# Two small reorderings in a TensorE-bound attention kernel: a piece of the last tile moved ahead, and keys computed by weight chunk in both branches

## Chip, cores, metric

One core of one Trainium2 chip. The metric is the device time of one execution in microseconds (us); lower is better. "PE" is the tensor engine, "ACT" ScalarE, "DVE" VectorE, "SyncE" the engine that issues most of the DMAs.

## The reference

Two linear-attention blocks A and B read the same x (2048 x 640, bf16), each with its own weights, and are mixed by a gate.

```python
g = sigmoid((x * gate_w).sum(-1, keepdims=True))
# for X in (A, B); H = 32 heads of 20:
q, k, v = split_heads(x @ wqkv)
phi = lambda t: where(t > 0, t + 1, exp(t)) + 1e-6
kv  = einsum("bhsd,bhse->bhde", phi(k), v);  z = phi(k).sum(over s)
o   = (phi(q) @ kv) / (phi(q) @ z + 1e-6)
out_X = o @ wo
out = g * out_A + (1 - g) * out_B
```

The kernel folds kv and wo into one 640 x 640 matrix per branch (WPA, WPB; "the projection"), so that the output of a tile of 128 rows is two products, one per branch, and the scaling by 1/den and by the gate goes onto phi(q). The folded matrix is written out to HBM and read back to get another layout.

## The kernel before

The program lists operations; a small list scheduler inside it picks the order on each engine other than PE from estimated times. PE keeps the program's order. Cuts are marked.

The loads at the start, all on the SyncE queue except x's tile 1 and small ones. `xt_dma` is a transposing load of x^T; x^T of tiles 0 and 1 is made by PE itself.

```python
ld_x("ACT", 1)
...
for c in range(NC):                 # NC = 5 chunks of 128 rows of the key weights
    if c == 0:
        ld_x("SP", c)
    ld_wk("SP", "A", c)             # 160 KB each
xt_dma(2, 3)
for c in range(NC):
    ld_wk("SP", "B", c)
for t0, t1 in ((3, 4), (4, 5), (5, 6), (6, 8), (8, 12), (12, 16)):
    xt_dma(t0, t1)
```

The keys. One `k_step` is one weight chunk for one tile: a matmul of 512 and one of 128 or 129 columns. `k_unit` is five steps and the evaluation of phi.

```python
warm(4); warm(1, 2)                 # matmuls on ones, to have PE busy
pss = [Buf("k", "ps", 2) for _ in range(2)]
x_tp(0); warm(1, 1); x_tp(1)        # x^T of tiles 0, 1 on PE
for c in range(2):
    for t in range(2):
        k_step("A", t, c, pss[t])
gate_col()
for c in range(2, NC):
    for t in range(2):
        k_step("A", t, c, pss[t])
...                                 # k_post of both
k_unit("A", 2)
for t in range(3):
    k_unit("B", t)
for t in range(3, NT):
    for X in XS:
        k_unit(X, t)
```

The end. A's part of tiles 0 to 14 is computed while B's projection is on its way, copied to SBUF, and later added to B's part. Tile 15 has both parts at the very end.

```python
for t in range(8, NOA): o_part(t)   # NOA = 15: A's parts; B's projection is being stored and loaded
...
for t in range(NOA): o_rest(t)      # B's parts, added to A's by DVE, stored
...
def out_last(t):                    # t = 15
    for lo, hi, eng in ((0, 512, "ACT"), (512, D, "DVE")):
        ps = Buf("o", "ps")
        for X in XS:
            o_mm(X, t, ps, lo, hi)
        o_post(t, ps, lo, hi, eng, ...)
```

## Time and profile before

| | before |
|---|---|
| time, median (range) of the first 3 runs | 188.17 us (188.03 to 188.83) |
| span of the profiled run | 186.8 us |
| PE busy | 184.0 us (98%) |
| DVE, ACT busy | 74%, 51% |
| PE's waits once the keys have begun | 0.35 us before B's weight chunks, 0.45 us before B's projection |

PE is nearly always busy, so only its short waits can be had. The prediction shows the lines and how the two numbers in the last row come out of the start times of matmuls. A busy share alone would have said that nothing is left.

### The profile page before, as it was taken

The page shows a single profiled execution, that of the slowest core. Times are in us where ns is not written, and L with a number is a line of the kernel's source. Part 1 is how long each engine was busy: PE and PEld are TensorE (multiplying, and loading weights), DVE is VectorE, ACT ScalarE, POOL GpSimd, SP SyncE. Part 2 cuts the span into 40 slices and gives each one's busy share as a digit, 9 for nine tenths or more (in the row PEclk, how much of TensorE's full clock was granted, in tenths as well). Part 3 has the DMA queues.
Part 4 walks back from the last instruction along what each step waited for, and adds up shares of the span by engine and source line. Part 5 has one row for each costly group of instructions (what it writes and reads, how often), then busy time and mean ns, then how long its engine had stood idle before and what let it go on. Part 6 is the DMA issues. An engine that isn't in the chain of part 4 may idle for free.

```text
span 186.8 us, 3273 instructions
## 1 busy us (share of the span) xinstructions
PE 184.0 (98%) x1297; PEld 106.6 (57%) x1297; DVE 137.4 (74%) x264; ACT 95.2 (51%) x167; POOL 0.8 (0%) x10
## 2 busy tenths in 40 slices
PE   9999999999999999999999999999999999999995
PEld 4555555555555556555557555555566555555552
DVE  2388888888833555487799999998899996368652
ACT  5455655556554546544675666887633775300001
POOL 1000000000000000000000000000000000000000
DMA  6999999994001011010701412025426256523433
GB/s 190 291 163 163 266 394 362 338 200 114 4 0 35 0 39 35 0 35 20 100 2 35 84 33 50 14 62 154 175 41 115 58 131 164 143 105 107 142 107 105
DMA packets 36501, 21.38 MB, mean 114 GB/s; under 512 B 25694, under 2 KB 36230, under 8 KB 36486
## 3 DMA queue, kind: packets, MB, share of 16 engines
q1 hardware_dynamic: 36044, 20.96, 44.4%
q8 instruction: 10, 0.16, 0.4%
q10 hardware_dynamic: 442, 0.21, 0.4%
q14 instruction: 5, 0.04, 0.1%
HBM read 10.87 MB, written 4.26 MB: 81 GB/s over the span
## 4 chain that ended last, share of the span: by engine, by line
PE 92%; DMA 4%; ACT 2%; issue 0%; DVE 0%; SPq 0%; DVEq 0%
PE ps L795 23%; PE ps L536 19%; PE ps L641 18%; PE ps L955 18%; PE ps L642 5%; PE ps L537 5%; DMA WPB<-wpsB 3%; DMA wpsB<-WKW 2%; PE ps L703 2%; PE ps L467 1%; ACT WKW L753 1%; PE ps L738 1%; ACT PKB L979 1%; PE ps L480 1%; DVE TSB L999 0%
## 5 line engine op out<-in xcount | busy, mean ns | idle before, releaser
L536 PE MATMUL ps<-WKW,XT 128*128 128x512 bf16 x160 | 44.6, 382 | 0.0
L812 ACT ACTIVATE EK<-ps 128x512 bf16<-128x512 f32 x40 | 23.9, 598 | 30.1 <-PE ps L795 29.9
L537 PE MATMUL ps<-WKW,XT 128*128 128x128 bf16 (+1 forms) x160 | 35.3, 220 | 0.0
L569 ACT ACTIVATE EK<-ps 128x640 bf16<-128x640 f32 x32 | 22.4, 704 | 10.3 <-DVE EK L572 5.4
L536 PEld LDWEIGHTS ps<-WKW,XT 128*128 128x128 bf16 x160 | 15.7, 98 | 19.6 <-DMA WKW<-in_B_wqkv_dram 0.7
L795 PE MATMUL ps<-XT,WQA 128*128 128x512 bf16 x100 | 24.5, 379 | 0.0
L795 PE MATMUL ps<-XT,WQB 128*128 128x512 bf16 x100 | 23.8, 380 | 0.0
L641 PE MATMUL ps<-XN,PKA 128*128 128x512 bf16 x80 | 23.5, 379 | 0.0
L641 PE MATMUL ps<-XN,PKB 128*128 128x512 bf16 x80 | 23.5, 379 | 0.0
L822 DVE TENSOR_SCALAR EK<-EK 128x512 bf16<-128x512 bf16 x40 | 11.6, 289 | 13.5 <-ACT EK L812 13.3
L642 PE MATMUL ps<-XN,PKA 128*128 128x129 bf16 x80 | 17.6, 220 | 0.0
L642 PE MATMUL ps<-XN,PKB 128*128 128x129 bf16 x80 | 17.6, 220 | 0.0
L955 PE MATMUL ps<-WPA,EX 128*128 128x512 bf16 x120 | 17.0, 299 | 0.0
L955 PE MATMUL ps<-WPB,PKA 128*128 128x512 bf16 x120 | 16.5, 299 | 0.3 <-DMA WPB<-wpsB 0.3
L795 PEld LDWEIGHTS ps<-XT,WQB 128*128 128x128 bf16 x100 | 10.9, 118 | 8.6 <-issue 0.4
L537 PEld LDWEIGHTS ps<-WKW,XT 128*128 128x128 bf16 x160 | 15.8, 98 | 0.0
L572 DVE TENSOR_SCALAR EK<-EK 128x640 bf16<-128x640 bf16 x32 | 10.4, 326 | 7.2 <-ACT EK L569 7.1
L795 PEld LDWEIGHTS ps<-XT,WQA 128*128 128x128 bf16 x100 | 10.6, 117 | 8.1
L641 PEld LDWEIGHTS ps<-XN,PKA 128*128 128x128 bf16 x80 | 9.4, 117 | 7.9
L641 PEld LDWEIGHTS ps<-XN,PKB 128*128 128x128 bf16 x80 | 9.4, 117 | 7.9
L580 DVE SCALAR_TENSOR_TENSOR PKA<-ps,EK 128x640 bf16<-128x640 f32 x16 | 13.2, 825 | 0.5
L580 DVE SCALAR_TENSOR_TENSOR PKB<-ps,EK 128x640 bf16<-128x640 f32 x16 | 13.2, 825 | 0.6
(77 smaller groups left out, 222.8 us busy)
## 6 DMA issues: line engine op xcount, KB each, us to landing
out_dram<-TSB SPq DMA_DIRECT2D x15, 160.0 KB, 1.8
XN<-in_A_x_dram SPq DMA_DIRECT2D x1, 2240.0 KB, 8.9
WKW<-in_A_wqkv_dram SPq DMA_DIRECT2D x5, 160.0 KB, 3.9
WKW<-in_B_wqkv_dram SPq DMA_DIRECT2D x5, 160.0 KB, 3.6
WQA<-in_A_wqkv_dram SPq DMA_DIRECT2D x1, 800.0 KB, 10.6
WQB<-in_B_wqkv_dram SPq DMA_DIRECT2D x1, 800.0 KB, 11.7
WVA<-in_A_wqkv_dram SPq DMA_DIRECT2D x1, 800.0 KB, 12.7
WVB<-in_B_wqkv_dram SPq DMA_DIRECT2D x1, 800.0 KB, 14.5
```

The costliest lines, as they stand in the source:

```text
L536: e.matmul(a[:, 0:512], l, WK[X][:, c, 0:512], start=(c == 0), stop=(c == NC - 1))
L537: return e.matmul(a[:, 512:w], l, WK[X][:, c, 512:w], start=(c == 0), stop=(c == NC - 1))
L569: op("ACT", lambda e: e.activation(EK[:, ek.slot, :], psw(ps, D), ACT.Exp), act_cost(D), ins=[ps] + first, outs=[ek], name="ke")
L572: lambda e: e.tensor_scalar(EK[:, ek.slot, :], EK[:, ek.slot, :], 1.0, EPS, op0=ALU.min, op1=ALU.add),
L580: lambda e: e.scalar_tensor_tensor(PKt[X][:, t, :], psw(ps, D), 0.0, EK[:, ek.slot, :], op0=ALU.max, op1=ALU.add),
L641: e.matmul(a[:, 0:512], l, XN[:, t, 0:512], start=(t == 0), stop=(t == NT - 1))
L642: return e.matmul(a[:, 512 : D + 1], l, XN[:, t, 512 : D + 1], start=(t == 0), stop=(t == NT - 1))
L703: r = e.matmul(PS[0:n, ps.slot, GR * i : GR * i + NC * w], WV[X][:, c, lo : lo + n], gv[:, c, :, 24 * u : 24 * u + w], start=(c == 0), sto ...
L795: r = e.matmul(PS[:, ps.slot, :], WQ[X][:, c, g::5], XT[:, c, 512 * b : 512 * b + 512], start=(c == 0), stop=(c == NC - 1),)
L812: lambda e: e.activation(EQ[:, eq.slot, :], PS[:, ps.slot, :], ACT.Exp),
L822: lambda e: e.tensor_scalar(EQ[:, eq.slot, :], EQ[:, eq.slot, :], 1.0, EPS, op0=ALU.min, op1=ALU.add),
L955: r = e.matmul(a[:, l0 - lo : h0 - lo], PQ[X, b][:, g, 128 * (t % 4) : 128 * (t % 4) + 128], WP[X][:, g, l0:h0], start=(X == first and g = ...
```

## The change

The intent: take both waits out without adding or removing a matmul. A's 512 columns of tile 15 (1.08 us of PE) fill the wait before B's projection. At the start, B's weights go ahead of x^T of tile 2, and B's tiles 0 and 1 share each chunk as it arrives, as A's did already.

```diff
         ld_wk("SP", "A", c)
-    xt_dma(2, 3)
     for c in range(NC):
         ld_wk("SP", "B", c)
-    for t0, t1 in ((3, 4), (4, 5), (5, 6), (6, 8), (8, 12), (12, 16)):
+    for t0, t1 in ((2, 3), (3, 4), (4, 5), (5, 6), (6, 8), (8, 12), (12, 16)):
         xt_dma(t0, t1)
@@ keys
-    k_unit("A", 2)
-    for t in range(3):
-        k_unit("B", t)
-    for t in range(3, NT):
+    pss = [Buf("k", "ps", 2) for _ in range(2)]
+    for c in range(NC):
+        for t in range(2):
+            k_step("B", t, c, pss[t])
+    for t in range(2):
+        k_post("B", t, pss[t])
+    for t in range(2, NT):
         for X in XS:
             k_unit(X, t)
@@ end
-    def out_last(t):
-        for lo, hi, eng in ((0, 512, "ACT"), (512, D, "DVE")):
-            ps = Buf("o", "ps")
-            for X in XS:
-                o_mm(X, t, ps, lo, hi)
+    LAST = ((0, 512, "ACT"), (512, D, "DVE"))
+    blast = [Buf("o", "ps") for _ in LAST]
+
+    def last_a(t):
+        o_mm("A", t, blast[0], 0, 512)
+
+    def last_b(t):
+        for (lo, hi, eng), ps in zip(LAST, blast):
+            if hi == D:
+                o_mm("A", t, ps, lo, hi)
+            o_mm("B", t, ps, lo, hi)
             o_post(t, ps, lo, hi, eng, "ACT" if hi == D else "SP")
@@ order
     for t in range(8, NOA):
         o_part(t)
+    last_a(NT - 1)
@@
-    out_last(NT - 1)
+    last_b(NT - 1)
```

## The prediction

> **What bounds the kernel now.** I read the page first, then the waits of the tensor engine (PE), then PE alone in order of time wherever a wait was named, then the SyncE queue and the landings beside those places.
>
> The page's first part, and from its groups the only PE group with an idle time in front of it:
>
> ```profile
> PE 184.0 (98%) x1297; PEld 106.6 (57%) x1297; DVE 137.4 (74%) x264; ACT 95.2 (51%) x167; POOL 0.8 (0%) x10
> L955 PE MATMUL ps<-WPB,PKA 128*128 128x512 bf16 x120 | 16.5, 299 | 0.3 <-DMA WPB<-wpsB 0.3
> ```
>
> PE is busy for 184.0 of 186.8 us; VectorE (DVE) has 74%, ScalarE (ACT) 51%. The rest of the span is the start (0.39 us) and what follows the last matmul (about 2.1 us, read off the order of time: last matmul done at 184.74, end at 186.8). So only two things can shorten this kernel: less PE work, or the short stretches in which PE waits. The change leaves the number and shapes of the matmuls as they are, so all of it must come from stretches. The list of waits names these for PE and its weight loads:
>
> ```profile
> PEld ps L536 <- DMA WKW<-in_B_wqkv_dram: 0.7, 2, 0.4
> PEld ps L536 <- DMA WKW<-in_A_wqkv_dram: 0.4, 1, 0.4
> PE ps L955 <- DMA WPB<-wpsB: 0.3, 1, 0.3
> ```
>
> Weight loads run beside matmuls, so their 0.7 us isn't 0.7 us of lost time. What was lost shows in the start times of the matmuls (first column; PE in order of time, second unit of keys of branch B):
>
> ```profile
> 8.97 0.38 PE L536 MATMUL ps<-WKW,XT 128*128 128x512 bf16 x1
> 9.19 0.22 PE L537 MATMUL ps<-WKW,XT 128*128 128x129 bf16 x1
> 9.43 0.39 PE L536 MATMUL ps<-WKW,XT 128*128 128x512 bf16 x1
> 9.66 0.22 PE L537 MATMUL ps<-WKW,XT 128*128 128x129 bf16 x1
> 9.86 0.39 PE L536 MATMUL ps<-WKW,XT 128*128 128x512 bf16 x1
> 10.09 0.22 PE L537 MATMUL ps<-WKW,XT 128*128 128x129 bf16 x1
> 10.14 0.38 PE L536 MATMUL ps<-WKW,XT 128*128 128x512 bf16 x1
> ```
>
> These are chunks 2, 3, 4 of B's tile 0 and chunk 0 of tile 1. An undisturbed chunk (512 and 129 columns) takes 0.27 us from start to start, as the steps before 8.97 do. Here the steps are 0.46, 0.43, 0.28: lost are 0.19 and 0.16, together **0.35 us**. The arrivals that the trace records agree: B's five weight chunks are complete at 7.73, 8.19, 8.62, 9.39 and 9.81, and the two late matmuls start at 9.43 and 9.86.
>
> The second place, PE where A's parts of the output end and B's begin:
>
> ```profile
> 156.97 4.24 PE L955 MATMUL ps<-WPA,PKA 128*128 128x512 bf16 x30
> 161.46 3.60 PEld L955 LDWEIGHTS ps<-WPB,PKA 128*128 128x128 bf16 x27 [0.58 <-issue]
> 161.49 3.69 PE L955 MATMUL ps<-WPB,PKA 128*128 128x512 bf16 x26 [0.28 <-DMA WPB<-wpsB]
> ```
>
> The 30 matmuls that start at 156.97 are A's parts of tiles 12 to 14. In the B stage one tile follows another every 1.36 us (the DVE adds start at 164.40, 165.76, 167.12), so the next matmul was due at 156.97 + 3 x 1.357 = 161.04. It starts at 161.49: **0.45 us** lost. The page says 0.28 because it counts a matmul as busy until it has drained, not until the next may start. The chain of waits shows what this matmul is held by:
>
> ```profile
> 152.88 3.61 DMA wpsB<-WKW
> ...
> 156.62 4.73 DMA WPB<-wpsB
> 161.35 0.14 issue
> 161.49 23.27 PE ps L955 x170
> ```
>
> Two transfers, out to HBM and back, hold B's folded projection until 161.35. After it PE has 23.27 us without a wait.
>
> **What the Trainium skill says.** "TensorE: Matmul & The Clock Gate", section "Wait — 56ns, not 53.3ns?": a warm matmul of N columns follows the one before after N / 2.4 GHz + 2.5 ns. That makes 215.8 ns for 512 and 55.8 ns for 128 columns, and 5 x (215.8 + 55.8) = 1.358 us a tile; the trace has 1.36. The same page's "Back-to-back issue gap" calls 131 ns the sustained spacing for N = 512, which this trace doesn't show; I go with the measured spacing. "DMA: Bandwidth & Descriptors", section "Issuing engines are not separate DMA queues": all issuing queues share the same 16 DMA engines. So moving one load behind others on SyncE doesn't create bandwidth, it only changes who is first. The trace agrees: the mean busy share over the first 10 us is 0.91, and A's last three chunks land 0.35 to 0.6 us apart. "PSUM — Partial Sum Buffer", section "Specifications (TRN2)": 8 banks. A tile of 640 columns takes a pair here, and four pairs is all there is.
>
> **The change part by part.**
>
> *1. x^T of tile 2 behind B's weights.* On SyncE the transposing load is issued from 2.81 to 4.13 us, B's five weight loads from 4.18 to 6.64. Taking it out of the way moves all five up by 4.18 - 2.81 = 1.37 us at the issue. Issue to landing was 3.4 to 3.7 us for them. In bytes only one load of 160 KB is passed, which took 0.67 us of landing time (A's last chunk complete at 6.33, x^T at 7.00), so I expect the chunks 0.7 to 1.4 us earlier: chunk 4 at 8.4 to 9.1 instead of 9.81, chunk 0 at 6.4 to 7.0 instead of 7.73.
>
> *2. Keys by weight chunk for tiles 0, 1 in B too.* Today PE does A0 and A1 by chunk (until 7.07), A2 (7.07 to 8.43), then B0. After the change B0 and B1 follow A1 at once, chunk by chunk. So B's chunk 0 is wanted 1.36 us earlier, at 7.07. But a chunk is then used by two tiles, 0.54 us per chunk instead of 0.27: chunks 0 to 4 are wanted at 7.07, 7.61, 8.16, 8.70, 9.25. Against estimated landings of at most 7.0, 7.5, 7.9, 8.7 and 9.1 (each 0.7 earlier than before) all five are in time, if barely at the late end. Both gaps go: -0.35 us. x^T of tile 2 is wanted after those ten steps, at 7.07 + 10 x 0.272 = 9.79. It is issued at about 5.3; before, issue to landing was 4.2 us for it, which makes 9.5; the bound by bytes is 9.81, when everything up to B's chunk 4 had landed in the old order. So it's in time or late by little: I set down +0.05 us. The key units' PSUM pairs: A0's is wanted again at 9.79 and was free once DVE had read it, at 8.93 (8.10 + 0.83). By the same rates (ACT 0.17 + 0.70, DVE 0.33 + 0.82 a unit) B0's is free near 11.7 and wanted at 12.5. No wait from there.
>
> *3. A's 512 columns of tile 15 ahead of B's first tile.* Five matmuls of 512 columns, 5 x 0.216 = 1.08 us, move from the tail (181.86 to 182.94 in the trace) into the wait for B's projection. PE then reaches B's first tile at 161.04 + 1.08 = 162.12 and finds the projection there (161.35 + 0.14). The tail loses 1.08 us, the stretch before gains 1.08 and loses its gap: net -0.45 us. I don't count 1.08. With part 2 the PE work and the projection's whole chain move earlier together by 0.3, since the chain starts from PE's own last small burst at 146.35; the slack of 162.12 - 161.49 = 0.63 us stays. The price is one bank held from there to the end, so B's 15 tiles have three pairs in place of four. An add takes 0.82 us and begins 0.1 us after its tile is done, and the pair is wanted again two tiles (2.7 us) later: even with a 0.81 us scaling ahead of it there's no wait.
>
> *The end.* The last three pieces keep their order: B's 512 columns, both branches' 128 columns, eviction, two stores. All of it moves forward unchanged.
>
> Sum: -0.35 + 0.05 - 0.45 = **-0.75 us** of 188.17, so **187.4 us**, 0.4% faster.
>
> **The rivals.**
>
> *A. The new load order only trades one wait for another.* B's first chunk is wanted at 7.07 now, and x^T of tile 2 comes 2.5 us later at the issue. For it: DMA is full in those microseconds, and margins are tenths. Against: the bytes ahead of B's chunks fall, and each chunk now feeds twice as much PE time. If chunks come only 0.4 earlier and x^T at 10.2, 0.3 to 0.5 us returns: 187.8.
>
> *B. The wait for B's projection is shorter or longer in other executions than in the profiled one.* The gain of part 3 is the gap, up to 1.08 us. If the gap is usually 0.1, gain 0.4 in all (187.75); if usually above 1.0, gain up to 1.4 (186.8). The three times lie 0.8 us apart, so such a variation can't be excluded.
>
> *C. Something is reshuffled.* The kernel's own list scheduler fixes the order on DVE, ACT and SyncE from simulated times; a small shift early, or a bank held late, can put a transposing load ahead of the stores of B's projection (such a load took 1.2 to 1.6 us of SyncE). Of that, 0.63 us is covered; the rest would show. Against: the order of the last transposes is pinned in the code. This would make 188.2 to 189.
>
> *D. The full 1.08 us comes off the tail.* It would if PE were idle for as long before B's first tile; the trace has 0.45. 186.8.
>
> **Range and chances.** The centre is 187.4. A with 15 to 20%, B either way with some 25%, C with 10% widen it to 186.9 to 188.1 for 8 in 10. A change of 2% is 3.8 us; no wait of PE in this trace adds up to that, and no rival costs it. Faster 0.01, same 0.98, slower 0.01.
>
> **What would show it.** Right: no step above 0.3 us between the key matmuls' starts from 7.07 to 12.5; five matmuls of A's projection on their own directly before the first with B's; no idle time before these; the B stage still at 1.36 us a tile; the last matmul done near 184.0. Wrong, and in what way: a weight load waiting for x^T near 9.8 (A), a first B tile that still waits for its projection (B or C), an add that PE waits for in the last 25 us (the held bank).

## The result, and the profile after

| | before | after |
|---|---|---|
| median (range) of 6 runs each | 188.20 us (188.03 to 188.83) | 188.01 us (187.62 to 188.41) |
| ratio, 95% interval | | 0.9987 (0.9966 to 1.0008) |
| span of the profiled run | 186.8 us | 186.7 us |

A ratio is the mean time of one kernel's runs over that of the other's of the same rounds, so not quite the ratio of the medians quoted. The time is inside the predicted range, but the difference is 0.25 us (means 188.30 and 188.05) where 0.75 was forecast, and the interval allows at most 0.64.

Yet the trace shows what was forecast. First PE's waits of the kernel after, the whole list; the one at the top is before the keys begin, the other is for x's tile 0. (ps is the accumulator in PSUM that is written, WKW the key weights, XT x^T; L466 is line 466 of that run's kernel, so the same statement is L535 in one kernel and L536 in another.)

```profile
PE ps L466 <- DVE ONE L383: 0.4, 1, 0.4
PE ps L479 <- DMA XN<-in_A_x_dram: 0.2, 1, 0.2
```

No weight chunk of B and no projection is waited for. PE in order of time where A's parts end and B's begin (start, duration, instruction, count):

```profile
157.23 5.32 PE L957 MATMUL ps<-WPA,PKA 128*128 128x512 bf16 x34
162.17 3.85 PEld L957 LDWEIGHTS ps<-WPB,PKA 128*128 128x128 bf16 x28
162.39 3.91 PE L957 MATMUL ps<-WPB,PKA 128*128 128x512 bf16 x27
```

A's tiles 12 to 14 are followed by the five extra matmuls (34 in the list: 35 less one record that is missing), and B's first matmul follows without an idle mark, 162.39 - 157.23 = 5.16 us later, which is 3 x 1.357 + 1.08 = 5.15. From A's tile 12 to the end of the last matmul it is 27.33 us, and 27.77 before: -0.44 us, as forecast (-0.45).

So the loss must be at the start. The first 512-column key matmuls of the kernel after:

```profile
3.84 0.63 PE L535 MATMUL ps<-WKW,XT 128*128 128x512 bf16 x1
4.38 0.63 PE L535 MATMUL ps<-WKW,XT 128*128 128x512 bf16 x1
4.91 0.63 PE L535 MATMUL ps<-WKW,XT 128*128 128x512 bf16 x1
5.44 0.63 PE L535 MATMUL ps<-WKW,XT 128*128 128x512 bf16 x1
6.05 0.39 PE L535 MATMUL ps<-WKW,XT 128*128 128x512 bf16 x1
```

A matmul that takes 0.63 us rather than 0.38 is read here as one at half clock: its step takes 0.53 us rather than 0.27. (The granted clock reads 1.00 all the same, so the durations are the only sign.) Here four are slow; in the trace before two were, at 3.65 and 4.18. That costs 2 x 0.26 = 0.52 us, and the keys began 0.19 us later (3.84 instead of 3.65), as x's first tile came later (2.58 instead of 2.39). In all, A's tiles 0 and 1 are done 0.59 us later than in the trace before (the weight load of the eleventh step, the first after them, starts at 7.63 instead of 7.04); it isn't the full 0.71 because PE had lost about 0.1 us there to A's own chunks. From there to the end the trace after is 0.76 us shorter, as forecast. The Trainium skill, "TensorE: Matmul & The Clock Gate", section "What's actually happening", says that PE's clock is released after a window of sustained work, that this window runs free of the kernel's start, and that the point of release varies by half a microsecond from run to run. The traces agree that it varies, but more widely (below).

Three theories of the front part followed. **Chance**: the clock's release is luck, equal for both kernels, and both gains are real in every run. **Absorbed**: weights arrive at fixed times, so a late clock lets them arrive unnoticed; the 0.35 us wait exists only in early-clock runs of the kernel before, and the front part of the change gains less on average. **Caused**: the change itself makes the start later.

### The profile page after: what moved, and what is told of

Same layout as the page of the kernel before. It is cut to its first block, busy times and chain, and to the rows that moved or that the text cites. A ratio compares the mean times of both kernels' runs of the same rounds, so it can differ in the third digit from the quotient of the medians.

```text
span 186.7 us, 3247 instructions
## 1 busy us (share of the span) xinstructions
PE 182.6 (98%) x1272; PEld 107.1 (57%) x1297; DVE 137.2 (73%) x264; ACT 95.0 (51%) x167; POOL 0.8 (0%) x10
## 4 chain that ended last, share of the span: by engine, by line
PE 97%; DMA 1%; issue 1%; DVE 0%; DVEq 0%
PE ps L957 23%; PE ps L797 23%; PE ps L535 18%; PE ps L643 18%; PE ps L536 5%; PE ps L644 5%; PE ps L705 2%; DMA XN<-in_A_x_dram 1%; PE ps L740 1%; PE ps L479 1%; DVE TSB L1001 0%; PE ps L466 0%; DVEq L237 0%; PE ps L516 0%
## 5 line engine op out<-in xcount | busy, mean ns | idle before, releaser
L535 PE MATMUL ps<-WKW,XT 128*128 128x512 bf16 x154 | 43.8, 386 | 0.0
L536 PE MATMUL ps<-WKW,XT 128*128 128x128 bf16 (+1 forms) x160 | 35.5, 222 | 0.3
L535 PEld LDWEIGHTS ps<-WKW,XT 128*128 128x128 bf16 x160 | 15.9, 99 | 19.1 <-issue 0.6
L797 PE MATMUL ps<-XT,WQA 128*128 128x512 bf16 x96 | 24.0, 379 | 0.1
L957 PE MATMUL ps<-WPA,EX 128*128 128x512 bf16 (+1 forms) x117 | 16.6, 297 | 0.2
L957 PE MATMUL ps<-WPB,PKA 128*128 128x512 bf16 (+1 forms) x118 | 16.4, 298 | 0.1
L536 PEld LDWEIGHTS ps<-WKW,XT 128*128 128x128 bf16 x160 | 15.9, 99 | 0.0
L579 DVE SCALAR_TENSOR_TENSOR PKA<-ps,EK 128x640 bf16<-128x640 f32 x16 | 13.2, 825 | 0.5
L579 DVE SCALAR_TENSOR_TENSOR PKB<-ps,EK 128x640 bf16<-128x640 f32 x16 | 13.2, 825 | 0.6
```

Source lines behind the costliest of these rows:

```text
L535: e.matmul(a[:, 0:512], l, WK[X][:, c, 0:512], start=(c == 0), stop=(c == NC - 1))
L536: return e.matmul(a[:, 512:w], l, WK[X][:, c, 512:w], start=(c == 0), stop=(c == NC - 1))
L579: lambda e: e.scalar_tensor_tensor(PKt[X][:, t, :], psw(ps, D), 0.0, EK[:, ek.slot, :], op0=ALU.max, op1=ALU.add),
L797: r = e.matmul(PS[:, ps.slot, :], WQ[X][:, c, g::5], XT[:, c, 512 * b : 512 * b + 512], start=(c == 0), stop=(c == NC - 1),)
L957: r = e.matmul(a[:, l0 - lo : h0 - lo], PQ[X, b][:, g, 128 * (t % 4) : 128 * (t % 4) + 128], WP[X][:, g, l0:h0], start=(X == first and g = ...
```

## The experiments

Sixteen runs, each with five timing rounds against the kernel before on the same chip. All results were correct.

### 1. Both kernels again, and each half of the change alone

No edit for `base_again` (the kernel before) and `chg_again` (the kernel after). `tail_only` has only the last two hunks of the diff (end, order), `front_only` only the first two (loads, keys).

> The kernel before, unchanged, to see how its start varies from one execution to the next. In the first trace two 512-column key matmuls ran at half speed (0.63 us each) and PE waited 0.35 us for B's weight chunks; in the trace after the change four ran at half speed (0.53 us more lost) and nothing waited. Theory 'chance' (the clock's release moves from run to run whatever the kernel; both gains are real): ratio 1.000, and among profiles of this kernel some show four half-speed matmuls. Theory 'absorbed' (the arrivals of the weights are fixed in time, so a late clock eats the 0.35 us gap of the kernel before): ratio 1.000, and where four matmuls are slow the gap before B's chunks is gone. Theory 'caused' (the change itself makes the start later): two slow matmuls here again.

Measured: 188.62 us, ratio 1.0007 (0.9982 to 1.0031). Its profile is a late-clock one: matmuls are slow until 6.36. And there is no wait for B's chunks. PE's only waits, complete:

```profile
PE ps L467 <- DVE ONE L383: 0.4, 1, 0.4
PE ps L955 <- DMA WPB<-wpsB: 0.3, 1, 0.3
```

The matmuls around its last slow one, and where B's chunks come in:

```profile
5.27 0.63 PE L536 MATMUL ps<-WKW,XT 128*128 128x512 bf16 x1
5.87 0.59 PE L536 MATMUL ps<-WKW,XT 128*128 128x512 bf16 x1
6.36 0.45 PE L536 MATMUL ps<-WKW,XT 128*128 128x512 bf16 x1
6.71 0.38 PE L536 MATMUL ps<-WKW,XT 128*128 128x512 bf16 x1
...
9.70 0.38 PE L536 MATMUL ps<-WKW,XT 128*128 128x512 bf16 x1
9.97 0.38 PE L536 MATMUL ps<-WKW,XT 128*128 128x512 bf16 x1
10.24 0.38 PE L536 MATMUL ps<-WKW,XT 128*128 128x512 bf16 x1
```

The steps at 9.70, 9.97, 10.24 have the undisturbed 0.27 us. B's chunks 3 and 4 landed at 9.51 and 9.91, as late as in the first trace (9.39, 9.81), but PE reached them later. This is the picture of "absorbed", and it takes "caused" away as the only reason: the kernel before has late starts too.

> The changed kernel, unchanged, in more rounds. 'chance': 0.75 us below the kernel before (ratio 0.996), and a profile with two slow matmuls may show up. 'absorbed': about 0.45 us below (ratio 0.9976), plus 0.35 us only in runs with an early clock. 'caused': about 0.2 us below (0.9987 as measured first), four slow matmuls again and the first key matmul at 3.84 rather than 3.65 us.

Measured: 187.89 us, ratio 0.9986 (0.9949 to 1.0023), no PE wait but for the first two. One of the six runs took 190.14 us; the other five average 187.86. The profiled run wasn't that one, so its reason stays unknown.

> Only A's 512 columns of the last tile ahead of B's first tile; the start is that of the kernel before. By the prediction -0.45 us (the gap before B's projection) in the profile, ratio 0.9976. In the trace after the change the projection came 0.20 us earlier in relation to PE's work, so the gap may vary: -0.25 to -0.45. 'chance' and 'absorbed' say the same here; 'caused' too, since the start isn't touched.

Measured: 188.02 us, 0.9979 (0.9961 to 0.9996). No wait for the projection, and 27.33 us from A's tile 12 to the last matmul again. At the start, B's chunks came late in this trace (the first at 8.53, the last at 10.26), and the steps of B's tile 0 lost 0.68 us to them.

> Only the new load order and the keys of tiles 0 and 1 by chunk in both branches; the old tail. 'chance': -0.35 us less 0.05 (ratio 0.9984). 'absorbed': 0 to -0.35 us by the clock of each run, -0.1 on average (0.9995). 'caused': +0.2 us or more (above 1.001), with a late first key matmul or four slow ones.

Measured: 188.26 us, 0.9989 (0.9968 to 1.001). An early-clock start (the second key matmul, at 4.24, is the last slowed one) without a wait for B's chunks. It showed the next bound: PE waits 0.37 us for A's chunk 1, which landed at 5.07:

```profile
4.24 0.45 PE L535 MATMUL ps<-WKW,XT 128*128 128x512 bf16 x1
...
5.12 0.39 PE L535 MATMUL ps<-WKW,XT 128*128 128x512 bf16 x1 [0.37 <-DMA WKW<-in_A_wqkv_dram]
```

### 2. More starts, and the front change taken apart

`base_third` and `chg_third` have no edit. `loads_only` and `keys_only` are the two halves of the front change:

```diff
# loads_only: the first hunk alone
-    xt_dma(2, 3)
...
+    for t0, t1 in ((2, 3), (3, 4), ...
# keys_only: the second hunk alone
-    k_unit("A", 2)
+    (B's tiles 0 and 1 by chunk)
```

> The kernel before once more, for the spread of its start. So far: one trace with an early clock (half speed until about 4.7 us) where PE waited 0.35 us for B's chunks and A's tile 3 began at 12.87, one with a late clock (until about 6.3 us), no wait, 13.24. 'absorbed' expects one of these two pictures or one in between, with A's tile 3 never before 12.8: its lower bound is the arrival of B's chunk 4 (9.8 to 9.9) plus eleven steps of 0.272 us. 'chance' expects wait and slow matmuls to occur independently of each other. Ratio 1.000 for both.

Measured: 188.39 us, 0.9994 (0.9974 to 1.0015). An early start (A's tile 3 at 12.75, by its first matmul, a little before the bound that I had stated, as the chunks came 0.1 earlier), a wait of 0.21 us for B's chunks, and a surprise at the end. Chain of waits and PE's list:

```profile
152.75 3.59 DMA wpsB<-WKW
...
156.48 5.43 DMA WPB<-wpsB
161.91 0.14 issue
```

```profile
PE ps L955 <- DMA WPB<-wpsB: 1.0, 1, 1.0
```

The same load of the projection took 5.43 us here and 4.73 in the first trace; PE lost 1.13 us. So the wait that the tail part removes isn't fixed. In the seven traces with the old tail and the old warm-up (this one, the first, and those of `base_again`, `front_only`, `loads_only`, `keys_only`, `front_second`) it was 0.17 to 1.13 us, 0.48 on the mean, taken as the time from A's tile 12 to the last matmul less the 27.32 that PE's work alone needs (3 x 1.357 + 23.25).

> The changed kernel once more. It has no wait for B's chunks, so its start follows the clock alone: A's tile 3 at 12.5 to 12.8 with an early clock, about 13.1 with a late one. 'absorbed': 0.45 us (tail) plus 0.1 to 0.3 us faster on average, ratio 0.9964 to 0.9972. 'chance': -0.8 us, 0.9957. 'caused' (dead if a clock as early as in the first trace of the kernel before shows up here): 0.9987. One run in six took 190.14 us last time, alone among 12; if this comes back in the changed kernel only, the change has a price in some executions that the medians hide.

Measured: 187.81 us, 0.9960 (0.9942 to 0.9978); A's tile 3 at 12.58. A start as early as the first trace's does occur in the changed kernel (eleventh step at 6.99, against 7.04): "caused" is dead. No run above 188.22.

> Only x^T of tile 2 moved behind B's weights; the keys stay A0, A1, A2, B0. A2 is due at 7.1 to 7.7 and x^T of tile 2 lands at 9.4, as in the changed kernel: PE waits 1.7 to 2.3 us there, and the 0.35 us before B's chunks is gone. All theories: slower by 1.5 to 2.0 us, ratio 1.008 to 1.011. That shows the two parts of the front change only pay together.

Measured: 190.20 us, 1.0085 (1.0065 to 1.0104), as expected. The two largest waits of PE:

```profile
PE ps L535 <- DMA XT<-in_A_x_dram: 1.9, 1, 1.9
PE ps L535 <- DMA WKW<-in_A_wqkv_dram: 0.4, 1, 0.4
```

The new load order alone moves the wait to x^T of tile 2 and makes it five times as long. It needs the new order of keys, which puts ten steps of other work ahead of it.

> Only the keys of tiles 0 and 1 by chunk in both branches; the loads keep the old order, so B's chunks come at 7.7, 8.2, 8.6, 9.4 and 9.8. B0 is due at 7.1 to 7.7 and the last pair of steps can't start before 9.8: A2 starts at 10.4 and A's tile 3 at 13.1 in an early-clock run (before: 12.87), 13.2 in a late one (as before). 'absorbed': the old order costs 0.25 us in early-clock runs and nothing in late ones: ratio 1.000 to 1.0015. 'chance': 1.0015.

Measured: 188.85 us, 1.0022 (1.0000 to 1.0045). PE's largest wait, in an early-clock run (only the first key matmul, at 3.84, is slow):

```profile
PE ps L536 <- DMA WKW<-in_B_wqkv_dram: 0.8, 1, 0.8
```

With the old load order B's tile 0 comes up before B's chunk 0 has arrived. A's tile 3 begins at 13.2 as in the late-clock `base_again`, but an early-clock start is the fair comparison: 12.87 in the first trace, 12.75 in `base_third`. So the half change costs 0.4 to 0.5 us here, where 0.25 was expected for an early clock; the time, 0.4 us more, agrees, though its interval just reaches 1.000.

### 3. A fourth copy, a spare load moved, and a later PE

```diff
# chg_cst (on the changed kernel)
-    dma("ACT", "cst", CST[:, :], cap[:, :], ...)      # before A's weight chunks
+    dma("SP", "cst", CST[:, :], cap[:, :], ...)       # behind the loads of x^T
# base_late, chg_late (on the kernels before and after)
     x_tp(1)
+    warm(6, 1)
```

> The changed kernel a fourth time, for the size of the gain. By the traces so far: front order new against old -0.24 us on the mean of four starts each (A's tile 3 at 12.5 to 13.1 against 12.7 to 13.3), tail -0.16 to -1.12, mean -0.48, so -0.7 us, ratio 0.9962. If the first measurement was the true size: 0.9987. No wait of PE for B's projection, A's first B tile 5.15 us after A's tile 12, as in every trace with the new tail.

Measured: 188.05 us, 0.9978 (0.9957 to 1.0000); A's tile 3 at 12.69, no wait of PE for B's chunks or the projection, but one of 0.45 us for A's chunk 2, which landed at 5.55.

> The changed kernel with the small load of constants (8 KB in 128 pieces of 64 bytes, first used after 90 us) moved from between A's weight chunks on the ACT queue to behind the loads of x^T. Between A's chunks 0 and 1 landings lie 1.1 to 1.8 us, between the others 0.4 to 0.7; in one early-clock start PE waited 0.37 us for chunk 1. If the small pieces cause that distance, chunk 1 lands up to 1 us earlier and early-clock runs gain up to 0.3 us: ratio to the changed kernel of the same rounds 0.9985 to 1.0. If not: same landings, same time.

Measured: 187.73 us, 0.9961 (0.9941 to 0.9981). A's chunk 1 landed at 4.63, 1.2 us after chunk 0 and inside the range of the others (3.92 to 5.38), and chunk 2 at 6.05, later than anywhere else, with a PE wait of 0.6 us. So in this one trace the distance is there without the constants. The time lies 0.3 us below `chg_fourth` with intervals that overlap nearly whole: no difference shown.

> The kernel before with six more warming matmuls of 128 columns ahead of the keys (0.64 us at half speed): PE reaches B's chunks 0.3 us later at the same clock, the loads stay as they are. 'absorbed': the wait for B's chunks is gone or under 0.1 us in the trace, even with an early clock, and the time rises by 0 to 0.3, 0.15 on average, though PE does 0.64 us more work: ratio 1.000 to 1.001. If the gap were PE's own and not the loads': +0.3 to 0.6, ratio 1.002 to 1.003.

Measured: 189.84 us, 1.0066 (1.0048 to 1.0084): far outside what I had expected. The trace tells two things apart. At the start "absorbed" holds: the clock was early (two slow matmuls), PE did 0.64 us more work before the keys (they begin at 4.30 instead of 3.65), the eleventh step came 0.38 us later (7.42 instead of 7.04), and yet A's tile 3 began at 12.92, against 12.87 in the first trace; steps 11 to 20 took 2.72 us, so no chunk of B held PE. The time was lost at the other end. Chain of waits:

```profile
152.94 5.10 DMA wpsB<-WKW
...
158.18 4.72 DMA WPB<-wpsB
162.90 0.14 issue
```

The store of the projection took 5.10 us instead of 3.6, and PE then lost 1.9 us (29.26 from A's tile 12 to the last matmul, less 27.32). It isn't the scheduler: the order of instructions on SyncE, ACT and DVE is the same as in the kernel before. Why the store takes longer I didn't settle. The run can't be used as a measure of the start by its time.

> The changed kernel with the same six warming matmuls. It has no wait to hide them in: +0.3 us over the changed kernel[...], so 0.9978 to 0.9982 to the kernel before, and the distance to the one with the late start is what the tail alone is worth, 0.45 us.

Measured: 188.51 us, 0.9998 (0.9976 to 1.0019). The same slow store; the extra matmuls of the new tail hid 1.08 us of some 1.8, and the list of waits has 0.6 us of PE waiting for the projection. Its time is as unusable for the start.

### 4. Which term was too large

`tail_only` and the changed kernel have the same tail, which waits for nothing, so they differ by the front term alone, without the noise of the projection. Repeats, no new edits.

> Repeat of the kernel with the new tail alone. -0.45 us to the kernel before, ratio 0.9976. Its trace: B's first tile 5.15 us after A's tile 12 without a wait; start as in the kernel before, either an early clock with a wait for B's chunks or a late clock without one, A's tile 3 at 12.7 to 13.3 us.

Measured: 188.06 us, 0.9973 (0.9955 to 0.9990). Stretch to the last matmul 27.33 us; early clock, wait for B's chunks 0.21 us.

> Repeat of the changed kernel. If the front is worth 0.30 us in every run: 0.3 below the tail kernels of these rounds, 0.9960 to the kernel before. If absorbed by a late clock in most runs: 0.1 below the tail kernels, 0.9971. A's tile 3 at 12.5 to 13.1 us.

Measured: median 188.09 us, 0.9972 (0.9955 to 0.9989) from five runs. The profiled one, a slow run, took 391.35 us and is left out; the last section comes back to it.

> A second repeat of the same, for the number of runs and one more trace of the old start: ratio 0.9976.

Measured: 188.16 us, 0.9975 (0.9956 to 0.9994). A late start (the last slowed key matmul is at 5.25, and A's chunk 2 landed only at 5.95), no wait for B's chunks, 27.33 us.

> Repeat of the new start with the old tail. Worth 0.30 us: ratio 0.9984. Mostly absorbed: 0.9995. Its trace has the wait for B's projection again, 0.2 to 1.1 us.

Measured: 188.55 us, 0.9990 (0.9966 to 1.0015). 27.70 us to the last matmul: the wait for the projection was back. The start was late (eleventh step at 7.58) with two slow matmuls only, because A's chunk 1 landed at 5.38.

### All traces side by side

Read from the order of time: the start of the weight load of the 11th key step (A's tiles 0 and 1 are done), how much longer than 2.72 us the next ten steps took, the start of the weight load of A's tile 3 (30 steps are done in either order; its first matmul, quoted above, starts 0.06 later), and the time from A's tile 12 to the end of the last matmul. All in us.

| start | kernel | 11th step | steps 11-20, excess | A's tile 3 | tile 12 to last matmul | span |
|---|---|---|---|---|---|---|
| old | before | 7.04 | 0.33 | 12.81 | 27.77 | 186.8 |
| old | base_again | 7.74 | 0.00 | 13.18 | 27.78 | 187.2 |
| old | base_third | 7.03 | 0.21 | 12.69 | 28.45 | 187.4 |
| old | tail_only | 7.13 | 0.68 | 13.26 | 27.33 | 186.9 |
| old | tail_second | 7.24 | 0.21 | 12.90 | 27.33 | 186.5 |
| old | tail_third | 7.69 | 0.00 | 13.10 | 27.33 | 186.7 |
| new | after | 7.63 | 0.00 | 13.07 | 27.33 | 186.7 |
| new | chg_again | 7.24 | 0.00 | 12.68 | 27.33 | 186.3 |
| new | chg_third | 6.99 | 0.09 | 12.52 | 27.33 | 186.1 |
| new | chg_fourth | 7.19 | 0.00 | 12.63 | 27.33 | 186.2 |
| new | front_only | 7.27 | 0.01 | 12.72 | 27.50 | 186.5 |
| new | front_second | 7.58 | 0.01 | 13.03 | 27.70 | 187.0 |

The 11th step comes at 7.31 on the mean of the old starts and at 7.32 of the new: no effect of the change on what goes before is seen. With the old order, the four early starts (up to 7.24) have a wait, the two late ones have none: 0.24 us on the mean of six. With the new order, hardly any start has one: 0.02. A's tile 3 begins 0.21 us earlier on the mean (12.99 and 12.78), with a spread of over 0.5 us in either group. With the new tail every one of these traces has 27.33.

What makes a start early or late is not the clock alone. In nine of the twelve traces (all but `base_again`, `after` and `chg_third`) the third or the fifth key step loads its weights 0.04 to 0.05 us after A's chunk 1 or 2 has landed, so it was this chunk that held it. A's chunk 1, issued at 0.91 us in all of them, landed anywhere from 3.92 (`chg_fourth`) to 5.38 us (`front_second`). `tail_third` and `front_second` were late by a chunk of A; `base_again` and `after` by half-speed matmuls.

And all runs together, over three chips at least, so with the chips' differences in them (mean, and 95% interval from resampling the runs):

| | runs | mean | against before |
|---|---|---|---|
| before | 52 | 188.53 | |
| new tail | 18 | 188.10 | -0.43 (-0.55 to -0.30) |
| new front | 12 | 188.34 | -0.19 (-0.44 to +0.08) |
| both, the change | 28 | 187.99 | -0.54 (-0.66 to -0.41) |
| both, with the run of 190.14 | 29 | 188.07 | -0.46 (-0.63 to -0.26) |
| both, against new tail | 28, 18 | | -0.11 (-0.24 to +0.02) |
| the same, with the run of 190.14 | 29, 18 | | -0.04 (-0.21 to +0.17) |

So the tail's gain is shown by times too. The front's is not: its interval holds zero, and on chip 10 alone, the one with the most runs of both kernels (11 and 12), it is -0.01 (-0.18 to +0.19).

## Why the prediction was right or wrong

**The bound and the two places: right.** PE set the time in every trace of both kernels, and no other engine took over.

**Part 3, the tail, -0.45 us: right, with more spread than I saw.** Measured -0.43 (-0.55 to -0.30). It was the first trace's gap that I used; other traces had 0.17 to 1.13. Rival B was real as a variation around the forecast. Rival D (the full 1.08 us) came near in one trace of the kernel before, the one with 1.13. Three pairs in PSUM for B's stage were enough: 22.18 us for it in every fast trace of the kernel after, which is 23.25 less the 1.08 moved away.

**Parts 1 and 2, the front, "Both gaps go: -0.35 us", with 0.05 for x^T: this step failed.** The term of -0.30 measured -0.11 (-0.24 to +0.02) by times, which is not clear of zero, and -0.21 by traces. The mechanism was right: the wait goes when the chunks come earlier, and x^T of tile 2 is in time (chunk 4 at 8.72, x^T at 9.41 in the trace after; 8.4 to 9.1 and 9.5 were forecast). It was wrong to count one execution's wait as every execution's. B's chunks arrive at times set by the DMAs; PE arrives when A's tiles 0 and 1 are done, and that is set by its half-speed matmuls and by the landing of A's own chunks. The wait is the difference, if positive. The profiled run of the kernel before had an early start. In a late one (two of six old starts) nothing is left to gain, and in an early one the change now runs at the pace of the clock or of A's chunks (0.37 us of wait in `front_only`, 0.45 in `chg_fourth`). `base_late` shows the same by force: 0.64 us more PE work ahead of the keys moved A's tile 3 by 0.05. That A's chunks can hold PE stood in a line which the prediction shows (0.4 us of weight loads waiting for them); it made no term of it.

**The sum.** -0.43 - 0.11 = -0.54 in place of -0.75 (a split of the -0.54, not a check of it). The first measurement, -0.25, was smaller than both: with six runs each, spread over 0.8 us, its interval reached -0.64. Of the missing 0.29, 0.23 lies in the six runs of the kernel before, which were good ones (mean 188.30 against 188.53 over all 52); whether by luck or by their chip isn't shown. The profile after was one with a late start. That a few runs spread by as much as the effect could be read from the three times of the kernel before (0.8 us); I used it to widen the range for the time, and not to doubt what six runs would show of the change.

**Rivals A and C.** No new wait took the old one's place (A): the ten steps after the 20th took 2.72 us in every new start, so x^T of tile 2 never held PE. The scheduler reshuffled nothing (C): beyond the keys of tiles 0 to 2 and the moved load, the listed orders on ACT, DVE and SyncE are those of the kernel before. A loss of the size that C feared did occur in `base_late` and `chg_late`, my own edits, but without any reordering.

**Left open:** the run of 190.14 us, and why the store of the projection took 1.5 us longer in the two late kernels.

## What to carry to other kernels

A wait in one trace is the difference of two arrival times, and each of them has its own spread: here a chunk of A that was issued at the same time landed 1.5 us apart in two traces, and the last half-speed matmul moved by 2.5 us. Read several traces, and count the wait only in the share of runs that have it. When waits are filled rather than shortened, the spread goes too, as far as the filling reaches: moving 1.08 us of independent matmuls into the wait for the projection made that stretch the same 27.33 us in every fast trace of the new tail but that of `chg_late`, where the wait was longer. An order of loads and the order of work that uses them change together or not at all: one half alone cost 1.7 us here, the other half 0.4.

## What the Trainium skill lacked or had wrong

- "TensorE: Matmul & The Clock Gate", section "What you observe": the release of the clock "around 4µs into sustained matmul activity, ±500ns run-to-run". Here PE is busy from 0.4 us, and the last slowed key matmul starts anywhere from 3.84 (`keys_only`) to 6.36 us (`base_again`), and in `base_third` and `loads_only` not even the first, at 3.85 and 3.81, was slow: a spread of 2.5 us or more, in which each key step done at half clock costs 0.26 us. The next section of that page does say that the count of slow matmuls varies by run, 6, 11 or 14 in one kernel.
- The same page, the caveats on the clock's records, know a clock stuck at a quarter for 50 us and more. In one execution of about 150 (`chg_fifth`, profiled) PE ran at about half speed for the whole run, 389.8 us, while the granted clock read 1.000. The durations show it: 679 ns a matmul against 386 in the trace after, while the longest groups of ScalarE and VectorE kept theirs (597 against 598 ns, and 825 in both). The span and granted clock of that run, and its costliest group (count, busy us, mean ns):

```profile
core 0: 389.8 us, clock 1.000
```

```profile
L535 PE MATMUL ps<-WKW,XT 128*128 128x512 bf16 x154 | 90.8, 679 | 0.0
```

- The same page, section "Back-to-back issue gap", gives 131 ns as the sustained spacing for 512 columns. Every fast trace here has 215 to 216 in its streams of weight load and matmul, the other formula of that page.
- No page has how much one and the same transfer varies within a kernel: the 800 KB load of B's projection took 4.73 us in one trace and 5.43 in another of the same kernel, its store 3.59 and 3.61. A's chunk 1, 160 KB issued at 0.91 us, landed from 3.92 to 5.38.
